# The first eight key and query blocks: from GpSimd's casting loads to fp32 loads on the SyncE and ScalarE queues

## The chip, the cores and the metric

The kernel runs on one core of a Trainium2 chip. A core has TensorE (PE in the profile; PEld is its loading of weights), VectorE (DVE), ScalarE (ACT), GpSimd (POOL) and SyncE (SP), which work side by side and wait for each other by semaphores. SP, ACT and POOL can each start transfers (DMAs) between the chip's memory and the on-chip memory. The metric is the time of one execution on the device in microseconds (us). Less is better.

## The reference, cut to what matters

An attention with 8 batches, 8 heads, 576 positions of 64 numbers, a window of 128 positions and a bias that falls with the distance, and then a two-layer network with a squared relu. Inputs and output are fp32.

```python
batch, n_heads, seq, head_dim = (8, 8, 576, 64)
n_tokens, d_model, d_ff = (4608, 512, 2048)
...
scores = scale * np.matmul(q, k.transpose(0, 1, 3, 2))
bias = slopes[:, None, None] * (-np.abs(rel).astype(np.float32))[None, :, :]
mask = (rel >= 0) & (rel < window)
scores = np.where(mask, scores + bias[None], -1000000000.0)
...
attn = np.exp(scores)
attn = attn / (np.sum(attn, axis=-1, keepdims=True) + 1e-09)
out = np.matmul(attn, v)
...
x = np.ascontiguousarray(attn_out.transpose(0, 2, 1, 3)).reshape(B * S, H * D)
h = x @ w_in
r = np.maximum(h, 0.0)
g = r * r
return (g @ w_out).astype(np.float32)
```

## The kernel before, in words

**Tiles.** All products run in bf16 with fp32 sums. The 4608 tokens are cut into 40 blocks, numbered by m: a block is 128 query positions of one batch (64 for the last of a batch) with all eight heads. For each block its keys and queries (tile kq, 128 positions by 2 x 512 numbers) and values are loaded, keys and queries are transposed (kqT, or kqf for the first four), scores, exponentials and the product with the values follow, the result x is normalized and transposed into xT. Blocks 0 to 3 are the first blocks of four batches. They have no block before them and are handled by `lone`, which adds the bias by a product with the identity. The later blocks multiply by a table of masks.

**Then the network.** Groups g of 512 tokens go through w_in (products h, relu on ACT, square on DVE or ACT, into g) and through w_out (products o, added up, stored). Group 0 and its neighbours are done in small units; later groups with a Strassen-like scheme of seven products, which needs sums of weights (us for w_in, wsum for w_out).

**Names of steps.** `lkq5` loads keys and queries of block 5 by POOL's queue, `lv5` its values; `w_in0` to `w_in4` and `w_out0` to `w_out3` are pieces of the weights, also by POOL's queue, and each casts from fp32 to bf16 on its way. `tp5.0` and `tp5.1` transpose the block's keys and queries on PE (blocks 0 to 7; later blocks by a DMA of SP, `kqT8` and on), `ev5.0.0` evacuates them from PSUM, `b`, `s`, `e`, `pv`, `r`, `n`, `xp`, `x` are a block's bias, scores, exponentials, product with the values, reciprocal, normalization, transposition and its evacuation. `u0.2.1` is the second piece of the w_in products of tokens 256 to 383 of group 0, `reluu0.2.1` and `squ0.2.1` what follows it; `o` are the w_out products of group 0.

**What sets the order.** The program is not ordered by the loops. Every step is a task with engines that may run it, and the string ORDER lists all tasks as they are emitted, with the engine chosen for each (:d DVE, :a ACT, :g POOL, :s SP, none PE) and the PSUM bank or buffer. An engine runs its own tasks strictly in this order, so whatever stands ahead of a task on its engine delays it. A queue's DMAs are issued in order too. Completions of DMAs are counted on eight counters for the two hardware queues and eight for POOL's, so that a DMA can also wait for the one that used its counter before.

**Around the change.** Block 0 alone is loaded otherwise (N_HW = 1): its keys and queries come as fp32 in four loads of 128 KB, `lk0.0`, `lk0.1`, `lq0.0`, `lq0.1`, on SP and ACT, each in runs of 256 numbers (1 KB), into a stage that lies in the memory of wsum before wsum is needed, and DVE casts them into kq (`ck0`, `cq0`). The position on a partition is another one there (four positions of a pair of heads lie together), which the evacuation after the transposition puts right. The source's pattern is

```python
if split:
    return s.rearrange("(c r) (g i) d -> g c r (i d)", r=2, i=4)
return s.rearrange("h s d -> s h d")
```

The load of blocks is at L551 to L600 (`source`, `load_block`), the transposition at L630 to L675 (`transpose_kq`).

Of the kernel before, what the change touches and what calls it, by code (L numbers as in the profile page):

```python
# [8 lines left out]
FP32 = mybir.dt.float32  # L9
# [8 lines left out]
N_HW = 1  # L18
# [24 lines left out]
NF = 8  # L43
UT = 1
# [6 lines left out]
RT = 4  # L51
# [10 lines left out]
s0 tp3.0::5 tp3.1::1 n1.1:d e0.0:a b3::7,0 ev3.1.0:a ev3.0.0:a xp1.0::3 s3 n2.0:d r2.1:d one0.0:d pv0.0::6  # L62
n2.1:d e0.1:a pv0.1::1 x1.0:a xp2.0::2 one0.3:d r0.0:d x2.0:a u0.1.0::5 r0.1:d n0.0:d n0.1:d xp0.0::4 u0.2.0::3
e3.0:a e3.1:a x0.0:d dist0:d u0.0.1::6 u0.0.0::2 pv3.0::1 pv3.1::7 one1.4:d r3.0:d n3.0:d r3.1:d one1.1:d n3.1:d
u0.1.1::0 u0.0.2::4 xp3.0::1 u0.2.1::7 x3.0:d mask1.2:a reluu0.1.1:a:0 reluu0.0.1:a:1 reluu0.2.0:a:2 squ0.0.1:d
squ0.2.0:d u0.3.0::0 reluu0.1.0:a:3 u0.2.2::6 reluu0.2.1:a:1 mask0.3:a reluu0.0.2:a:2 squ0.2.1:d reluu0.2.2:a:1
squ0.2.2:d squ0.1.0:d u0.3.1::3 w_out3:g o0.2.0::1 tp4.0::5 tp4.1::7 squ0.1.1:d one1.7:d ev4.1.0:d squ0.0.2:d
reluu0.3.0:a:1 mask1.5:a mask0.5:a mask1.6:a mask0.6:a reluu0.0.0:a:3 ev4.0.0:a one1.3:d squ0.0.0:d u0.1.2::4
reluu0.1.2:a:0 reluu0.3.1:a:2 us3.0:d one1.0:d u0.0.3::6 reluu0.0.3:a:3 one1.8:d u0.3.2::0 s4::2,7,5,4 mask0.2:a
mask1.3:a mask0.4:a mask0.0:a mask1.0:a e4.0:a e4.3:a squ0.1.2:d squ0.0.3:d mask0.1:a mask1.7:a mask1.1:a  # L70
mask0.7:a reluu0.3.2:a:0 squ0.3.0:d squ0.3.2:d u0.2.3::3 reluu0.2.3:a:3 mask1.4:a one1.6:d squ0.2.3:d e4.1:a
# [24 lines left out]
S2.1.1:d S4.1.1:d S3.1.1:d u2.0.7::6 u2.0.6::2 squ2.0.5:a reluu2.0.6:a:3 e13.2:a reluu2.0.7:a:0 m13.3:d lv16:g
lkq17:g lkq20:g x12:s x10:s x11:s u2.0.4::3 p1.5.0::5 reluu2.0.4:a:1 p1.5.1 s14::4,2,7,6 s5_1:a:5 e14.0:a
e14.1:a e14.2:a m13.2:d m13.0:d m13.1:d S4.1.0:d p1.6.0 pv13.0::3 u2.0.3::4 squ2.0.6:d squ2.0.4:d us1.1:d
m14.1:d r13.0:d m14.2:d n13.0:d m14.0:d reluu2.0.3:a:3 e14.3:a reluu2.0.1:a:1 squ2.0.0:a squ2.0.7:d p1.6.1
pv13.1::2 p1.3.0 r13.1:d n13.1:d m14.3:d s2_1:a:6 s15::7,3,4,6 pv14.0::1 pv14.1::2 r14.0:d r14.1:d us0.1:d  # L100
n14.0:d n14.1:d squ2.0.3:d lv15:g lkq18:g lkq19:g lv17:g lv18:g p1.7.0 p1.7.1 e15.0:a e15.3:a e15.2:a e15.1:a
s16::7,6,1,4 m15.0:d e16.0:a u2.1.2::2 e16.1:a e16.2:a reluu2.1.2:a:0 e16.3:a kqT17:s kqT20:s st1.2.1:s x14:s
x13:s kqT19:s u2.1.0::3 m15.1:d pv15.0::7 u2.1.3::6 reluu2.1.3:a:2 reluu2.1.0:a:3 c22_1:d us0.3:d m16.0:d
m15.2:d m15.3:d pv15.1::1 m16.1:d pv16.0::2 r16.0:d n16.0:d squ2.0.1:d r15.0:d r15.1:d p1.4.0 u2.0.2::4
u2.1.1::6 n15.0:d m16.3:d n15.1:d s17::3,2,7,1 reluu2.0.2:a:1 squ2.1.0:a m16.2:d pv16.1::4 squ2.0.2:d r16.1:d
# [224 lines left out]
def kernel(  # L330
    ctx: ExitStack, tc: tile.TileContext, q, k, v, moe_w_in, moe_w_out, out
):
    nc = tc.nc

    B, H, S, D = q.shape
    d_model = moe_w_in.shape[0]
# [9 lines left out]
    FCB = d_ff // 128  # L346
# [1083 lines left out]
```

## Time and profile before

| | |
|---|---|
| median of three runs | 294.59 us (294.20 to 294.94) |
| profiled execution | 293.89 us, of which the span from first to last instruction is 292.1 |
| PE busy | 282.8 us, 97% of the span |
| DVE, ACT, POOL busy | 247.1, 226.9, 106.5 us |
| granted clock of PE | 1.0 in every slice |
| read from memory | 36.70 MB |
| written to memory | 9.44 MB |
| POOL's queue | 115184 packets, 18.10 MB |
| SP's hardware queue | 54800 packets, 20.26 MB |

The span counts from the first instruction of the program. "Busy" of an engine is the time in which one of its instructions was running; a matmul's end is modelled. In lines of the timeline, the first number is the start and the second the duration; a line with SPq or ACTq is the issue of a transfer by that queue, whose landing comes later; a part in brackets is the idle time of the engine before the line and what ended it. A line number such as L572 is one of the kernel before.

### The profile page before, as it was taken

The page shows a single profiled execution, that of the slowest core. Times are in us where ns is not written, and L with a number is a line of the kernel's source. Part 1 is how long each engine was busy: PE and PEld are TensorE (multiplying, and loading weights), DVE is VectorE, ACT ScalarE, POOL GpSimd, SP SyncE. Part 2 cuts the span into 40 slices and gives each one's busy share as a digit, 9 for nine tenths or more (in the row PEclk, how much of TensorE's full clock was granted, in tenths as well). Part 3 has the DMA queues.
Part 4 walks back from the last instruction along what each step waited for, and adds up shares of the span by engine and source line. Part 5 has one row for each costly group of instructions (what it writes and reads, how often), then busy time and mean ns, then how long its engine had stood idle before and what let it go on. Part 6 is the DMA issues. An engine that isn't in the chain of part 4 may idle for free.

```text
span 292.1 us, 8683 instructions
## 1 busy us (share of the span) xinstructions
PE 282.8 (97%) x3443; PEld 238.5 (82%) x3443; DVE 247.1 (85%) x645; ACT 226.9 (78%) x445; POOL 106.5 (36%) x132
## 2 busy tenths in 40 slices
PE   5889999999999999999999999999999999999994
PEld 2589766788888888888888888888898888888884
DVE  4444588877798699999999999999999898999883
ACT  3658967688789695899999999899886957858710
POOL 8954377393265372912573630820000000000000
PEclk9999999999999999999999999999999999999999
DMA  9999999999999999999999999998500523010225
GB/s 124 166 199 195 190 167 179 145 130 141 180 167 143 179 207 171 131 139 173 185 173 141 142 197 154 168 168 139 116 3 5 152 80 91 1 41 20 90 81 154
DMA packets 170921, 39.64 MB, mean 136 GB/s; under 512 B 156928, under 2 KB 170368, under 8 KB 170880
## 3 DMA queue, kind: packets, MB, share of 16 engines
q0 software_dynamic: 115184, 18.10, 95.1%
q1 hardware_dynamic: 54800, 20.26, 37.6%
q10 hardware_dynamic: 896, 0.72, 1.0%
q8 instruction: 27, 0.44, 0.6%
q14 instruction: 14, 0.11, 0.1%
HBM read 36.70 MB, written 9.44 MB: 158 GB/s over the span
## 4 chain that ended last, share of the span: by engine, by line
PE 87%; DMA 8%; POOL 4%; issue 0%; ACT 0%; DVE 0%; POOLq 0%
PE o L1221 33%; PE h L1059 26%; PE h L965 13%; PE pv L816 6%; PE s L711 5%; DMA vf<-in_v_dram 3%; DMA kqT<-kq 3%; PE o L1137 2%; DMA kq<-in_q_dram 2%; POOL kq L590 2%; POOL vf L597 1%; POOL w_in_sb L535 1%; PE o L1323 1%; PE xp L865 0%; PE tp L653 0%
## 5 line engine op out<-in xcount | busy, mean ns | idle before, releaser
L734 ACT ACTIVATE P<-s 128x512 bf16<-128x512 f32 x120 | 65.6, 612 | 5.2 <-PE s L711 4.9
L1221 PEld LDWEIGHTS <-g 128*128 128x128 bf16 x624 | 60.0, 98 | 7.0
L590 POOL DMA_DIRECT2D kq<-in_k_dram x39 | 33.9, 868 | 69.4 <-DMA kqT<-kq 65.6
L932 ACT ACTIVATE rt<-h 128x512 bf16<-128x512 f32 (+1 forms) x73 | 42.3, 600 | 14.7 <-PE h L965 9.9
L1080 DVE TENSOR_TENSOR rt<-h,f 128x512 bf16<-128x512 f32 x72 | 48.7, 686 | 4.1 <-PE h L1059 1.3
L924 ACT ACTIVATE g<-rt 128x512 bf16<-128x512 bf16 x80 | 48.9, 636 | 1.4 <-DVE rt L1085 0.7
L1221 PE MATMUL o<-w_out_sb,g 128*128 128x256 bf16 x384 | 47.7, 273 | 0.0
L965 PE MATMUL h<-xT,w_in_sb 128*128 128x128 bf16 (+1 forms) x512 | 46.4, 246 | 0.0
L443 ACT ACTIVATE f<-h 128x512 f32<-128x512 f32 x59 | 34.9, 606 | 11.1 <-PE h L1059 10.9
L965 PEld LDWEIGHTS <-w_in_sb 128*128 128x128 bf16 x512 | 38.9, 98 | 3.9
L1059 PE MATMUL h<-xT,w_in_sb 128*128 128x256 bf16 x288 | 41.4, 273 | 0.1
L1059 PEld LDWEIGHTS <-w_in_sb 128*128 128x128 bf16 x384 | 35.8, 98 | 5.2 <-issue 0.3
L742 DVE TENSOR_TENSOR P<-P,masks 128x512 bf16<-128x512 bf16 x96 | 37.1, 420 | 2.2 <-ACT P L734 2.1
L597 POOL DMA_DIRECT2D vt<-in_v_dram x36 | 30.8, 876 | 16.6 <-PE pv L816 9.0
L590 POOL DMA_DIRECT2D kq<-in_q_dram x39 | 33.7, 865 | 5.7 <-DMA w_out_sb<-in_moe_w_out_dram 2.3
L926 DVE TENSOR_TENSOR g<-rt 128x512 bf16<-128x512 bf16 (+1 forms) x65 | 26.1, 415 | 6.9 <-ACT rt L932 6.6
L845 DVE TENSOR_TENSOR x<-pv,rec 128x256 bf16<-128x256 f32 (+1 forms) x80 | 31.4, 414 | 0.5
L1221 PE MATMUL o<-wsum,sums 128*128 128x256 bf16 x256 | 31.7, 273 | 0.0
L1221 PE MATMUL o<-wsum,g 128*128 128x256 bf16 x240 | 30.5, 273 | 0.0
L1059 PEld LDWEIGHTS <-us 128*128 128x128 bf16 x288 | 27.1, 98 | 3.7
L1087 ACT ACTIVATE rt<-rt 128x512 bf16<-128x512 bf16 x38 | 24.1, 637 | 5.6 <-DVE rt L1080 5.2
L816 PEld LDWEIGHTS <-P 128*128 128x128 bf16 (+1 forms) x576 | 24.0, 100 | 5.0 <-issue 2.3
(81 smaller groups left out, 398.3 us busy)
## 6 DMA issues: line engine op xcount, KB each, us to landing
out_dram<-f SPq DMA_DIRECT2D x54, 128.0 KB, 2.6
kq<-in_k_dram POOLq DMA_DIRECT2D x31, 128.0 KB, 5.9
kq<-in_q_dram POOLq DMA_DIRECT2D x31, 128.0 KB, 6.5
vt<-in_v_dram POOLq DMA_DIRECT2D x28, 128.0 KB, 7.0
w_out_sb<-in_moe_w_out_dram POOLq DMA_DIRECT2D x4, 512.0 KB, 14.5
w_in_sb<-in_moe_w_in_dram POOLq DMA_DIRECT2D x3, 512.0 KB, 10.2
out_dram<-f SPq DMA_DIRECT2D x4, 256.0 KB, 5.0
out_dram<-f SPq DMA_DIRECT2D x13, 64.0 KB, 2.1
```

The source lines that it names most:

```text
L443: nc.scalar.activation(o, i, AF.Copy)
L590: nc.gpsimd.dma_start(view(kq[s_kq[m].idx], i), source(src, m, split))
L597: nc.gpsimd.dma_start(tile_of(s_v[m])[0:n, :, 0:D], source(v, m))
L734: nc.scalar.activation(flat(Pt[sP.idx]), sS[i].tile.rearrange("p (j t) -> p j t", j=2)[:, :, lo:hi], AF.Exp, bias=0.0, scale=scale)
L742: nc.vector.tensor_tensor(flat(Pt[sP.idx]), flat(Pt[sP.idx]), flat(masks), op=ALU.mult)
L816: nc.tensor.matmul(sv.tile[0:n, hi * (D + 1):(hi + 1) * (D + 1)], prob, tile_of(s_v[mk])[:, h, 0:D + 1], start=mk == parts[0][1], stop=mk ...
L924: nc.scalar.activation(o, i, AF.Square, bias=0.0, scale=1.0)
L932: nc.scalar.activation(rts[srt.idx][:, 0:n], slot.tile[:, 0:n], AF.Relu, bias=0.0, scale=1.0)
L965: nc.tensor.matmul(slot.tile[:, f * w:(f + 1) * w], w_in_sb[:, cc, fc * 128:(fc + 1) * 128], xT[:, cc, lo % (XR * 128):lo % (XR * 128) + w ...
L1059: nc.tensor.matmul(slot.tile[:, j * 256:j * 256 + 256], a, b_, start=fresh and j == 0 and c == 0, stop=c == 1, skip_group_check=True)
L1080: nc.vector.tensor_tensor(rts[srt.idx], slot.tile, other(), op=ALU.add)
L1221: nc.tensor.matmul(slot.tile[:, z * 256:z * 256 + 256], stationary(c), moving(c), start=fresh and z == 0 and c == 0, stop=c == F - 1, skip ...
```

## The change

The blocks 0 to 7 are now all loaded as block 0 was: 32 loads of 128 KB in fp32, on SP's or ACT's queue, whichever ORDER names. There are four stages instead of one, in the four quarters of wsum; block m uses stage m % 4, so block 4 can be loaded when block 0's casts are done. The casts may run on DVE or ACT. POOL's queue keeps the values, the weights, and the keys and queries from block 8 on. The evacuation of the transposed blocks 1 to 7 takes the order of positions that only block 0 had. ORDER is new from beginning to end: block 1 is now first, then 2, 0 and 3, and the later work has other places, engines and banks.

```diff
-N_HW = 1
+N_HW = 8
...
 ORDER = """
-lk0.0:s iota:g ident:d dist1:d slope1.0:d slope0.3:d one0.1:d lk0.1:a lkq2:g warm0:d slope1.1:d warm::0 lkq1:g
-lq0.0:s slope1.3:a slope1.2:a slope0.2:a ck0:d slope0.0:a slope0.1:a lq0.1:a one0.2:d tp0.0::1 tp2.0::2 tp2.1::3
-ev2.0.0:d ev2.1.0:d tp1.0::4 ev1.0.0:a tp1.1::5 b2::6,7 s2 ev1.1.0:a b1::0,2 s1 b0::3,4 e2.0:a e2.1:a e1.0:a
-e1.1:a ev0.0.0:a cq0:d tp0.1::5 lv2:g pv2.0::6 r2.0:d ev0.1.0:d lv1:g lkq3:g lv0:g w_in0:g w_in1:g w_in2:g lv3:g
-w_in3:g w_out0:g lkq4:g w_in4:g w_out1:g w_out2:g lkq5:g lv4:g pv1.0::7 pv1.1::0 pv2.1::2 r1.1:d r1.0:d n1.0:d
...
+lk2.0:a iota:g ident:d dist1:d slope1.1:d warm0:d lk1.0:s lq1.0:s lq1.1:a lk1.1:a lv0:g warm::0 slope0.3:d
+lk3.0:s lk3.1:s lk0.0:s lv1:g slope1.0:d slope0.2:a slope0.0:a slope0.1:a ck1:d cq1:d ck3:d one0.1:d slope1.3:a
+slope1.2:a b0::1,2 tp1.0::3 tp1.1::4 ev1.0.0:d b1::5,6 tp3.0::7 ev3.0.0:d lk2.1:a lk0.1:a lq2.0:a lv2:g lq2.1:s
+lq0.0:s lq3.1:a lq0.1:a lq3.0:s ck2:d cq2:d ev1.1.0:a s1 e1.0:a b2::0,3 ck0:a e1.1:a pv1.0::4 r1.0:d one0.2:d
+n1.0:d cq0:d tp2.0::7 tp2.1::5 tp0.0::6 tp0.1::4 ev2.0.0:a ev2.1.0:a cq3:a s2 pv1.1::7 ev0.0.0:d ev0.1.0:d
+r1.1:d n1.1:d w_in1:g w_in0:g w_in2:g lv3:g w_in3:g lk4.0:s lq4.1:s lq4.0:s lk4.1:s w_in4:g w_out0:g w_out1:g
+e2.0:a e2.1:a tp3.1::5 ev3.1.0:d s0 pv2.0::6 e0.0:a e0.1:a b3::4,0 pv2.1::7 r2.0:d one0.0:d n2.0:d r2.1:d n2.1:d
+xp1.0::3 pv0.0::5 s3 x1.0:a pv0.1::1 xp2.0::6 u0.1.0::2 r0.0:d n0.0:d r0.1:d n0.1:d xp0.0::7 one0.3:d x0.0:d
+e3.0:a x2.0:a e3.1:a reluu0.1.0:a:0 lk5.0:a mask1.5:a u0.2.0::3 dist0:d u0.0.1::5 u0.0.0::4 pv3.1::1 pv3.0::6
+lk5.1:s mask0.4:a reluu0.0.0:a:1 mask1.4:a u0.0.2::0 u0.1.1::2 r3.0:d r3.1:d n3.0:d n3.1:d xp3.0::7 squ0.1.0:d
+x3.0:d u0.2.1::4 ck4:d u0.3.1::6 u0.3.0::1 lk6.0:s lq6.0:s lq5.0:s lq5.1:s mask1.3:a reluu0.2.0:a:2
...
-    stages = [wsum.rearrange("p s c t -> p (s c t)")[:, 0:4 * d_model].bitcast(FP32)]
+    stages = [x.rearrange("p c t -> p (c t)").bitcast(FP32) for x in (wsum[:, i] for i in range(4))]
...
         if split:
-            s_st = Slot("stage")
             t_l = []
+            s_st = Slot(f"stage{m % 4}")
             for i, src in enumerate((k, q)):
-                for r, (eng, e) in enumerate((("SP", nc.sync), ("SP", nc.sync) if m else ("ACT", nc.scalar))):
-                    def fetch(i=i, src=src, r=r, e=e):
-                        e.dma_start(view(stages[s_st.idx], i)[:, r], source(src, m, split)[:, :, r])
+                for r in range(2):
+                    def fetch(i=i, src=src, r=r):
+                        e = nc.scalar if t_l[2 * i + r].eng == "ACT" else nc.sync
+                        e.dma_start(view(stages[m % 4], i)[:, r], source(src, m, split)[:, :, r])
...
             def cast_kq(i):
                 w = slice(i * d_model, (i + 1) * d_model)
                 copy((c_k, c_q)[i],
                      kq[s_kq[m].idx][:, w].rearrange("s (i r d) -> s r i d", i=4, d=D),
-                     stages[s_st.idx][:, w].rearrange("s (r i d) -> s r i d", r=2, d=D))
-            engs = {"DVE": 350.0, "ACT": 480.0} if m else {"DVE": 350.0}
+                     stages[m % 4][:, w].rearrange("s (r i d) -> s r i d", r=2, d=D))
+            engs = {"DVE": 350.0, "ACT": 480.0}
```

More of the change, by code (lines that the diff above doesn't have):

```diff
@@ L62 @@
[L62 to L71, printed above, removed]
@@ L97 @@
[L97 to L105, printed above, removed]
-p1.4.1 e17.0:a n16.1:d e17.3:a e17.2:a reluu2.1.1:a:1 m17.2:d squ2.1.1:d m17.3:d kqT18:s st1.2.0:s x15:s
@@ new lines @@
+pv12.0::6 r12.0:d n12.0:d m12.2:d squ1.1.4:a reluu1.1.6:a:2 u2.0.6::1 reluu2.0.6:a:1 squ1.1.3:a us0.1:d S1.1.0:d
+u2.0.5::2 squ1.1.6:a S1.1.1:d S2.1.0:d S4.1.0:d S2.1.1:d s13::7,4,5,3 u2.0.0::1 e13.0:a e13.1:a reluu2.0.5:a:0
+reluu2.0.0:a:3 u2.0.4::6 reluu2.0.4:a:2 e13.2:a squ2.0.0:d e13.3:a p1.5.0::7 p1.5.1 m13.2:d s5_1:d:5 m13.1:d
+s14::4,2,1,6 pv12.1::5 r12.1:d n12.1:d m13.0:d e14.0:a e14.1:a squ2.0.5:a e14.3:a lkq17:g lv16:g lv15:g lv17:g
+lkq20:g x11:s x10:s x12:s S4.1.1:d p1.6.0 u2.0.7::3 reluu2.0.7:a:3 squ2.0.7:a pv13.0::4 m14.0:d r13.0:d m14.1:d
@@ new lines @@
+f7.0.2::2 p6.2.0::5 f7.0.5::0 c11.7.0:d:1 s1_6:a:1 sqc12.6.2:a reluc22.6.3:a sqc22.6.3:a st5.2.1:s x35:s
+st5.7.2:s p6.2.1 f7.0.6 s5.7.0:a:0 st5.4.2:s st4.3.0:s st5.7.3:s st5.4.3:s x37:s sqc12.6.3:d S1.6.1:d S2.6.0:d
+ut7.2:d n36.1:d c11_6:d S2.6.1:d S4.6.1:d f7.1.5::1 f7.0.3 s5.7.1:a:6 s2.7.0:a:4 S4.6.0:d c12.7.0:d:3 S3.6.1:d
+st5.3.0:s x36:s st4.3.1:s x38:s st5.3.1:s p6.5.0::2 f7.1.1::3 p6.5.1 st5.2.0:s st6.2.1:s s1.7.1:a:2 p6.6.0
+f7.1.2::5 f7.0.7 f7.1.6 c11.7.1:d:2 S3.6.0:d reluc11.7.0:d reluc12.7.0:a s2.7.1:a:4 sqc12.7.0:a s5_6:a:2
```

278 lines of the change are left out of this document (141 added, 137 removed).

## The prediction

> **What bounds the kernel now.** I read the page's first part, then the windows of the first 50 us, then the chain, the timeline of the start, and the DMA slices of the first 12 us. The page:
>
> ```profile
> PE 282.8 (97%) x3443; PEld 238.5 (82%) x3443; DVE 247.1 (85%) x645; ACT 226.9 (78%) x445; POOL 106.5 (36%) x132
> ```
>
> PE leaves 9.3 us of the span idle. The windows (us; busy of PE, PEld, DVE, ACT, POOL; clock; DMA share; GB/s) say where:
>
> ```profile
> 0.00:5.00 5.00, 2.19 (x6) 0.82 (x7) 2.65 (x10) 2.39 (x6) 4.20 (x10) 1.00 0.71 107
> 5.00:10.00 5.00, 3.52 (x38) 2.21 (x36) 1.69 (x3) 0.78 (x2) 5.00 (x6) 1.00 2.18 157
> 10.00:15.00 5.00, 4.72 (x71) 3.08 (x70) 2.63 (x11) 4.36 (x9) 5.00 (x8) 1.00 1.92 174
> 15.00:20.00 5.00, 4.30 (x79) 4.08 (x80) 1.88 (x8) 3.00 (x7) 2.30 (x4) 1.00 1.45 197
> 20.00:25.00 5.00, 4.87 (x91) 4.87 (x91) 2.54 (x9) 3.13 (x7) 2.44 (x3) 1.00 1.51 194
> 25.00:30.00 5.00, 5.00 (x80) 4.46 (x77) 2.70 (x12) 4.25 (x12) 2.56 (x4) 1.00 1.39 203
> ```
>
> From 25 us on PE is full, so only the first 20 us (and the tail, whose steps stay) can be won. In the chain, the last link of the start is the load of the fourth value block, v3, issued at 11.50 and 8.59 us on its way:
>
> ```profile
> 11.50 8.59 DMA vf<-in_v_dram
> ```
>
> The timeline shows what PE had done when that load let it go on:
>
> ```profile
> 0.74 0.69 SPq L572 DMA_DIRECT2D wsum<-in_k_dram  x1
> 0.74 0.68 ACTq L572 DMA_DIRECT2D wsum<-in_k_dram  x1
> ...
> 3.29 0.57 ACTq L572 DMA_DIRECT2D wsum<-in_q_dram  x1
> ...
> 3.79 0.59 DVE L441 CAST kq<-wsum 128x512 bf16<-128x512 f32 x1 [0.48 <-DMA wsum<-in_k_dram]
> ...
> 7.83 0.92 DVE L441 CAST kq<-wsum 128x512 bf16<-128x512 f32 x1
> ...
> 16.55 1.06 PE L965 MATMUL h<-xT,w_in_sb 128*128 128x128 bf16 x16
> ...
> 17.66 1.95 PE L965 MATMUL h<-xT,w_in_sb 128*128 128x128 bf16 x32
> ...
> 20.13 0.40 PE L816 MATMUL pv<-vf,P 128*128 128x65 bf16 x8 [0.52 <-DMA vf<-in_v_dram]
> ```
>
> At 20.13 the four lone blocks but for block 3's values product, and 48 h matmuls (u0.1.0, u0.2.0, u0.0.1, u0.0.0), are behind PE. The new order has the same list ahead of pv3.1. So the change is worth the shift of this one point, when PE passes pv3, plus whatever goes wrong later. The DMA slices of 0.3 us (window 0 to 12):
>
> ```profile
> GB/s 0 0 0 0 0 0 0 82 273 324 249 226 114 122 167 134 142 139 161 170 184 158 147 173 157 154 155 155 154 155 154 155 155 155 154 155 155 154 155 152
> ```
>
> Fp32 loads of the two hardware queues reach 324 GB/s alone; POOL's casting loads run at 155 GB/s (bytes as written), and the window from 12 to 30 us shows 200 to 210 GB/s where weights move. The engines are never empty after 2.1 us.
>
> **The change part by part, and the sum.**
>
> *POOL.* It loses 14 issues of 0.87 us (12.2 us). Its queue is now v0, v1, v2, w_in1, w_in0, w_in2, v3: three issues of some 0.9 from 1.34 and three w_in issues 0.73 apart put v3's issue at 6.3 instead of 11.50. Behind it stand seven transfers instead of thirteen.
>
> *SP and ACT.* 32 loads of 128 KB instead of 4. SP takes 23: 21 more at 0.58 are 12.2 us on a queue that is otherwise idle until the store at 43.57, so nothing waits but these loads. ACT takes 9, 7 more at 0.57 (4.0 us). Three go out by 2.6; then the table load (1.28, to 3.85) and five slope copies (1.2, to 5.05), then five more loads to 7.9. Only then can ACT start the first evacuation (ev1.1.0), against 8.93 before.
>
> *Casts.* 16 instead of 2: 10 more on DVE at 0.59 to 0.92 (5.9 to 9.2 us), 4 on ACT at the 0.60 of its evacuations (2.4 us). DVE is idle for 21 us and ACT for 17 of the first 50 (windows above and their continuation), which covers them; if it didn't, they would add to engines that are 95% busy from 120 to 200 us. Taken at nothing, except on the chain below.
>
> *The chain of the lone blocks.* Landing takes 2.8 to 3.0 us early, 4.4 once POOL's loads run (ACT's q load, issued 3.29, cast at 7.83). Block 2's k half goes out at 5.05, block 0's at 5.6, block 2's q half at 6.2, block 3's at 6.8, block 0's q half at 7.3: landed 9.4, 10.0, 10.6, 11.2, 11.7. DVE casts block 0's q to 12.4 (r1.0 and n1.0, 0.6 us, stand ahead of it). ACT then runs ev1.1, e1.0, ck0 (from 10.0), e1.1, ev2.0, ev2.1, cq3, two e2, two e0, x1.0 at 0.6 each: it is the busy engine, and x1.0 ends at 16.0. u0.1.0 starts at 16.0 (16.55 before); x2.0 ends at 17.2; u0.2.0, u0.0.1, u0.0.0 (0.89 per 16 matmuls) end at 19.0. By this chain alone PE would pass pv3 at 19.0, 1.1 us earlier.
>
> *v3's landing.* What must have been moved: four v at 0.846 (131 KB at 155 GB/s), 3.4 us; three w_in pieces, 1.05 MB at 205 GB/s, 5.1 us; 16 k and q loads at 0.405 (131 KB at 324 GB/s). Up to 3.6 us some 346 KB (five slices) are gone, 2.6 loads; 13.4 are left, 5.4 us. Sum from 3.6: 17.5. But loads of blocks 4 to 7 no longer stand behind the weights in POOL's queue. SP issues the first when block 0's k is cast (10.6), the second when its q is (12.4), then one each 0.58, and each lands some 4.4 us later whatever POOL has queued: in this trace ACT's load, issued at 3.29 after two of POOL's and while its third was being issued, took 4.4, while POOL's own k loads of the window from 12 to 30 us took a median of 13.5. Nine are issued by 16.5 and landed by 21, 3.6 us more: v3 lands at 21.1 instead of 20.09.
>
> The price of 0.405 is a lower bound: in the six slices from 5.4 to 7.2 us, where ACT's load of 131 KB ran beside POOL's, the total was 139 to 184 GB/s; 298 KB moved where POOL alone moves 279, so it took 0.72 us from POOL. Stores beside POOL's loads later in the trace are no dearer than 0.4. I take 0.405, since it is the rate of queued loads, as these are, and that row is of a single one; the upper end is kept (17.5 becomes 21.7 and n loads cost 0.72 each: eight land by then, 27.5, +7.4).
>
> The Trainium skill (DMA: Bandwidth & Descriptors, "Issuing engines are not separate DMA queues") states that DMAs of all engines run on the same 16 DMA engines and that spreading them saves the sequencer's time only. The trace agrees (139 to 184 GB/s together, 155 alone); by that rule the sum is the bytes' time, as above, and the 12.2 us saved on POOL are worth nothing.
>
> *After pv3.* w_in3 follows with 2.55 and seven more loads (2.8): 26.5. PE needs it for u0.2.2 5.9 us after 21.1 (pv 0.46, five h groups at 0.89, xp 0.39, tp 0.61): 27.0. Covered by 0.5 us. ACT's load of block 5 waits in the built program for the landing of SP's load of block 6 (a shared completion counter): issued 15, landed 19.3; behind it on ACT are masks and the relus that free the banks. PE needs the first of these banks (u0.2.1) after two h groups and xp3, 2.7 us past pv3; not seen in the sum, a loss of up to 1 us if the load takes 7.
>
> *The new order of the rest.* PE's idle time after 25 us is under 0.3 us before, so no gain; the loss is open where DVE has 19.5 to 19.9 of 20 us. Between 0.3 gained and 2 lost I take 0, as the products and buffers are the same.
>
> Sum: 21.1 - 20.1 = +1.0 us. The profiled execution took 293.89 (span 292.1 and 1.8 around it), which would become 294.9; the median of the runs, 294.59, lies 0.7 above it: 295.6.
>
> **The rivals.**
> *Chain sets it (faster).* v3 lands by 19.0: this needs blocks 4 to 7 to stay behind (at most three of them ahead: 17.5 + 1.2). For it: SP waits for casts and completions before it issues. Against: nothing else stands in SP's queue. It decides below 20.1, and gives 293.5.
> *Contended price.* Each load takes 0.72 of POOL's time throughout. For it: the only slices with both kinds of loads. Against: it is one load at a ramp. At 0.55, the middle, v3 lands near 24.4: 298.9; at the end, 302.
> *Nothing.* POOL's queue gets more turns, chain and landing balance near 20.1: 294.6. This is also the case that the move of queues does nothing because the transfers bound both kernels.
>
> **How the numbers follow.** v3 late by about 1 (0.4 to 2.5): 0.46, 295.6. Chain: 0.23, 293.5. Contended: 0.15. Nothing: 0.16. A change under 0.3% (0.9 us) can't be told from none here. Faster by more: 0.23 of the chain case and some order luck, 0.24; same: the nothing case and a little of the first, 0.19; slower: the rest, 0.57. The range leaves out the far end of the contended case and order luck below the chain: 293.2 to 299.0.
>
> **What would show it.** Right: pv3 waits for the DMA of vf, PE idles some 2 us near 19 to 21, block 5 or 6 loads land before v3, x1.0 ends near 16. Wrong: vf lands by 19; or PE waits earlier, for a cast or for ACT's evacuations past 17; or PE shows idle slices after 30 us, where I have none; or w_in takes the place of v3.

## The result, and the profile after

The changed kernel takes 304.17 us (median of six runs, 302.55 to 305.26); the kernel before took 294.76 beside it (293.64 to 295.80). The ratio is 1.0314 (1.0272 to 1.0356): slower by 9.4 us, where 1.0 had been forecast, and above the end of the forecast range, 299.0. The profiled execution took 305.08 us, 11.2 more than the one before.

The first part of the page of the changed kernel, and the line of its second part that gives the clock granted to PE in 40 slices of 7.6 us:

```profile
PE 287.7 (95%) x3432; PEld 241.2 (80%) x3432; DVE 253.3 (84%) x661; ACT 225.5 (74%) x443; POOL 94.2 (31%) x118
PEclk9999699999999999999999999999999999999999
```

PE is busy 4.9 us longer with 11 instructions fewer, and one slice, the fifth, has a lower clock. The windows (busy time and instructions of PE, PEld, DVE, ACT, POOL; clock; DMA share; GB/s) show the stretch:

```profile
5.00:10.00 5.00, 3.62 (x15) 1.59 (x14) 1.90 (x5) 0.48 (x3) 4.35 (x6) 1.00 1.64 227
10.00:15.00 5.00, 2.77 (x35) 1.98 (x34) 1.61 (x4) 2.48 (x5) 1.67 (x3) 1.00 1.29 256
15.00:20.00 5.00, 4.03 (x67) 2.89 (x67) 3.95 (x14) 3.71 (x8) 1.71 (x3) 1.00 1.43 210
20.00:25.00 5.00, 4.92 (x95) 4.79 (x91) 3.29 (x14) 2.35 (x5) 0.19 (x1) 1.00 1.20 237
25.00:30.00 5.00, 0.94 (x17) 0.82 (x15) 1.05 (x4) 0.82 (x4) 0.00 (x0) 0.88 1.18 244
30.00:35.00 5.00, 5.00 (x48) 4.99 (x48) 1.04 (x3) 3.50 (x11) 0.00 (x0) 0.50 1.20 254
```

From 25 to 30 us PE does almost nothing (17 instructions), and from 30 to 35 it is full but finishes 48, at half the clock. From 25 to 30 us the other engines are all but idle too; only the DMA works. The chain of the first 40 us says on what (start, length, what):

```profile
3.40 6.57 DMA wsum<-in_k_dram
...
9.99 6.39 DMA wsum<-in_q_dram
...
16.46 0.44 DVE kq L442
...
19.45 9.04 DMA wsum<-in_k_dram
...
28.59 0.54 ACTq L574
...
29.59 0.37 ACT rt L933
...
30.00 5.28 PE h L966 x48
```

Two things stand here. First, lq0.1 lands at 16.37, and the cast behind it opens the way for block 0. It stands in ACT's queue and was issued only at 9.99, when lk0.0, whose completion counter it shares, had landed (3.40 + 6.57 = 9.97). Second, a load of SP, lk6.0 (issued 19.45), lands only after 9.04 us, and what it lets go is ACT's load lk5.0, whose completion counter it shares. Behind lk5.0 on ACT stand the masks and the relus that free PE's banks. The timeline of ACT (start, length, engine, line, what; the idle time before it and its releaser in brackets):

```profile
21.79 0.60 ACT L933 ACTIVATE rt<-h 128x512 bf16<-128x512 f32 x1
28.59 0.54 ACTq L574 DMA_DIRECT2D wsum<-in_k_dram  x1
29.18 0.51 ACT L482 ACTIVATE masks<-sums 128x128 bf16<-128x128 f32 x2 [6.78 <-DMA wsum<-in_k_dram]
29.59 0.36 ACT L933 ACTIVATE rt<-h 128x256 bf16<-128x256 f32 x1
```

and that of PE over the same time:

```profile
23.53 0.41 PE L817 MATMUL pv<-vf,P 128*128 128x65 bf16 x8
...
30.00 5.28 PE L966 MATMUL h<-xT,w_in_sb 128*128 128x128 bf16 x48 [4.06 <-ACT rt L933]
35.08 0.89 PE L655 MATMUL tp<-ident,kq 128*128 128x128 bf16 x8
```

So pv3 is passed at 23.53 us instead of 20.13 (+3.4), then PE stands for 4.06, and the 48 matmuls after that take 5.28 instead of 2.84 (the same group at full clock, in the runs below): 9.9 us. tp4, the transposes of block 4, is a good mark for it. In the kernel before it began at 26.82:

```profile
26.82 0.61 PE L653 MATMUL tp<-ident,kq 128*128 128x128 bf16 x8
```

There PE had 16 h matmuls (0.89) and four o matmuls (0.87) more behind it than the new order has at this point, so the mark is 25.1 by the new order's list; now it begins at 35.08. The last 1.2 us come later; 0.53 of them are idle time of PE from 120 to 125 us.

### The profile page after: what moved, and what is told of

Read it like the earlier page. It is cut to its first block, busy times and chain, and to the rows that moved or that the text cites. A ratio compares the mean times of both kernels' runs of the same rounds, so it can differ in the third digit from the quotient of the medians.

```text
span 303.1 us, 8692 instructions
## 1 busy us (share of the span) xinstructions
PE 287.7 (95%) x3432; PEld 241.2 (80%) x3432; DVE 253.3 (84%) x661; ACT 225.5 (74%) x443; POOL 94.2 (31%) x118
## 4 chain that ended last, share of the span: by engine, by line
PE 86%; DMA 10%; SPq 2%; DVE 0%; issue 0%; ACT 0%; ACTq 0%; DVEq 0%
PE o L1222 31%; PE h L1060 25%; PE h L966 13%; PE pv L817 6%; PE s L712 5%; DMA wsum<-in_k_dram 5%; PE o L1138 5%; DMA xT<-x 2%; DMA wsum<-in_q_dram 2%; SPq L574 2%; PE tp L655 1%; PE o L1324 1%; PE xp L866 0%; ACTq L574 0%; DVE kq L442 0%
## 5 line engine op out<-in xcount | busy, mean ns | idle before, releaser
L592 POOL DMA_DIRECT2D kq<-in_k_dram x32 | 27.4, 856 | 99.9 <-DMA kqT<-kq 72.8
L933 ACT ACTIVATE rt<-h 128x512 bf16<-128x512 f32 x73 | 42.6, 602 | 16.2 <-PE h L966 7.1
L966 PE MATMUL h<-xT,w_in_sb 128*128 128x128 bf16 (+1 forms) x512 | 49.2, 254 | 4.1 <-ACT rt L933 4.1
L925 ACT ACTIVATE g<-rt 128x512 bf16<-128x512 bf16 x82 | 50.2, 644 | 0.9 <-DVE rt L1086 0.4
L966 PEld LDWEIGHTS <-w_in_sb 128*128 128x128 bf16 x512 | 41.0, 102 | 8.1 <-issue 4.2
L1060 PEld LDWEIGHTS <-w_in_sb 128*128 128x128 bf16 x384 | 35.4, 98 | 4.8
L927 DVE TENSOR_TENSOR g<-rt 128x512 bf16<-128x512 bf16 (+1 forms) x63 | 25.3, 412 | 7.6 <-ACT rt L933 7.1
L817 PEld LDWEIGHTS <-P 128*128 128x128 bf16 (+1 forms) x576 | 24.7, 101 | 5.7 <-issue 2.5
L1088 ACT ACTIVATE rt<-rt 128x512 bf16<-128x512 bf16 x36 | 22.7, 639 | 8.7 <-DVE rt L1081 8.6
L592 POOL DMA_DIRECT2D kq<-in_q_dram x32 | 27.6, 862 | 1.1 <-DMA vt<-in_v_dram 1.0
```

The source lines that it names most:

```text
L592: nc.gpsimd.dma_start(view(kq[s_kq[m].idx], i), source(src, m, split))
L817: nc.tensor.matmul(sv.tile[0:n, hi * (D + 1):(hi + 1) * (D + 1)], prob, tile_of(s_v[mk])[:, h, 0:D + 1], start=mk == parts[0][1], stop=mk ...
L925: nc.scalar.activation(o, i, AF.Square, bias=0.0, scale=1.0)
L933: nc.scalar.activation(rts[srt.idx][:, 0:n], slot.tile[:, 0:n], AF.Relu, bias=0.0, scale=1.0)
L966: nc.tensor.matmul(slot.tile[:, f * w:(f + 1) * w], w_in_sb[:, cc, fc * 128:(fc + 1) * 128], xT[:, cc, lo % (XR * 128):lo % (XR * 128) + w ...
L1060: nc.tensor.matmul(slot.tile[:, j * 256:j * 256 + 256], a, b_, start=fresh and j == 0 and c == 0, stop=c == 1, skip_group_check=True)
```

## The experiments

Theory A: ACT's stop at lk5.0 (head of line: one load with a late counter, relus behind it) and the clock that falls behind it cost some 6 us. Theory A2: the rest is the first chain, late because the loads of blocks 0 to 3 divide the DMA with what GpSimd's queue moves; A3 extends this to blocks 4 to 7. Rivals: the DMA as a whole is the cost and a moved load changes nothing (B), or the new order of all other work is (C). Columns: first w_in matmul (h), landing of the last of the sixteen loads of blocks 0 to 3, start of tp4 (us, profiled execution); median, what it is above the kernel before that ran beside it, and the ratio's interval.

| run | first h | sixteen | tp4 | median | above before | interval of the ratio |
|---|---|---|---|---|---|---|
| before | 16.55 | | 25.1 (see above) | 294.8 | | |
| changed | 20.62 | 16.37 | 35.08 | 304.17 | 9.4 | 1.027 to 1.036 |
| e1 | 21.18 | 16.08 | 29.01 | 298.20 | 3.4 | 1.009 to 1.018 |
| e2 | 20.53 | 16.28 | 32.30 | 302.24 | 7.5 | 1.023 to 1.030 |
| e3 | 22.07 | 16.55 | 33.04 | 302.22 | 7.5 | 1.021 to 1.030 |
| e4 | 21.37 | 16.11 | 29.37 | 297.91 | 3.2 | 1.008 to 1.015 |
| e5 | 20.19 | 15.95 | 28.12 | 298.99 | 4.1 | 1.010 to 1.017 |
| e6 | 21.26 | 15.95 | 29.14 | 300.74 | 5.8 | 1.017 to 1.021 |
| e7 | 22.21 | 16.92 | 30.05 | 301.73 | 6.8 | 1.016 to 1.027 |
| e8 | 17.67 | 12.90 | 31.26 | 300.94 | 6.2 | 1.018 to 1.030 |
| e9 | 19.72 | 13.28 | 28.45 | 300.43 | 5.7 | 1.015 to 1.023 |
| e10 | 22.00 | 16.73 | 29.84 | 298.70 | 4.0 | 1.011 to 1.017 |
| e11 | 19.11 | 13.54 | 29.00 | 300.15 | 4.8 | 1.010 to 1.023 |
| e12 | 17.65 | 13.09 | 27.74 | 298.94 | 3.6 | 1.005 to 1.016 |
| e13 | 16.89 | | 24.91 | 296.55 | 1.8 | 1.004 to 1.008 |
| e14 | 20.52 | 14.91 | 28.52 | 298.48 | 3.7 | 1.008 to 1.017 |
| e15 | 16.45 | | 25.68 | 296.27 | 1.1 | 1.002 to 1.007 |
| e16 | 20.05 | | 30.27 | 300.68 | 5.5 | 1.016 to 1.023 |

First h, landings, tp4 and all waits come from the one profiled execution of a run, which in e4, e7 and e12 took 2.6, 1.3 and 2.4 us more than the median.

**ACT's stop and the clock: e1, e10, e2.** e1 moves one load to SP's queue:

```diff
-... reluu0.1.0:a:0 lk5.0:a mask1.5:a ...
+... reluu0.1.0:a:0 lk5.0:s mask1.5:a ...
```

> One thing against the changed kernel: the load lk5.0 goes to SyncE's queue (it stands ahead of lk5.1 there), so that ScalarE's queue has no load behind block 3. Theory A (head of line: in the changed kernel ScalarE stood 6.78 us at lk5.0, for the landing of lk6.0 on a shared completion counter; its reluu tasks came late, TensorE idled 4.06 us, and the granted clock then fell to 0.50 for 5 us): the 4.1 us and the 2.4 us that 48 matmuls took longer both go, and the kernel takes 297 to 299 us; no idle of TensorE over 1 us between 25.5 and 30 us, granted clock over 0.85 in 30 to 35. Rival B (the loads of blocks 4 to 7 share the DMA with the weights, and something else of theirs then waits just as long): the wait moves to another row, and the kernel stays within 1 us of 304. Rival C (the new order of the rest costs the time): 302 to 304, with the idle spread over later slices.

Measured 298.20, within A's range. The windows of e1, to be set against the two of the changed kernel:

```profile
25.00:30.00 5.00, 5.00 (x93) 5.00 (x91) 3.02 (x9) 3.90 (x12) 0.30 (x1) 1.00 1.19 244
30.00:35.00 5.00, 5.00 (x98) 4.79 (x96) 2.92 (x9) 3.75 (x12) 3.22 (x4) 1.00 1.21 247
```

DMA share and GB/s are nearly the same as before the move; PE and the clock are full. One letter in the order is worth 6.0 us, and B and C fall as explanations of that part. e10 asks whether it was ACT's queue or the counter. The load stays on ACT, but stands ahead of e2.0 and so gets another counter:

```diff
-lk4.0:s lq4.1:s ... e2.0:a ... reluu0.1.0:a:0 lk5.0:a mask1.5:a
+lk4.0:s lk5.0:a lq4.1:s ... e2.0:a ... reluu0.1.0:a:0 mask1.5:a
```

> One thing against the changed kernel: lk5.0 stays in ScalarE's queue, but five activations earlier, ahead of e2.0 instead of behind reluu0.1.0. It then takes the completion counter of a load that landed near 11.5 us (lk2.1's), where the changed kernel's lk5.0 waited for lk6.0's, which landed at 28.5. Theory A (the stop is the wait for that counter, not a load in ScalarE's queue as such): ScalarE does not stop over 1 us between 16 and 30 us, TensorE does not idle there, and the kernel takes 297 to 299.5 us, as with lk5.0 on SyncE's queue. Rival (any load that ScalarE issues in this stretch stops it, because the ring is full): 301 us or more, with a wait of ScalarE of 3 us or more at the new place.

Measured 298.70, within A's range. ACT issues the load at 15.96 us, between two short pieces of work (the timeline of e10):

```profile
15.79 0.60 ACT L444 ACTIVATE kqf<-tp 128x512 bf16<-128x512 bf16 x1 [0.37 <-PE tp L655]
15.96 0.54 ACTq L574 DMA_DIRECT2D wsum<-in_k_dram  x1
16.28 0.62 ACT L444 ACTIVATE kq<-wsum 128x512 bf16<-128x512 f32 x1
```

So the wait on lk6.0's counter at that place was the cost, not a load in ACT's queue as such. e2 leaves the wait and fills PE's gap:

```diff
-x3.0:d u0.2.1::4
+x3.0:d idle::1 u0.2.1::4      # idle: 18 matmuls 128x512 on zeros, result unread
```

> One thing against the changed kernel: ahead of u0.2.1, the first matmul group that waits for ScalarE's late reluu0.0.0, 18 matmuls of 128x512 on zeros go into a free bank, which nothing reads. They last about as long as the idle stretch (3.9 us at 216 ns each) and leave the wait where it is. Theory A (the clock fell because TensorE idled): the idle of 4.06 us is filled, the wait for ScalarE stays and ends at 30.0 us as before, but the 48 matmuls behind it take 2.7 us and not 5.28, and the kernel takes 301.5 to 302.5 us. Rival B (the clock fell for another reason, the load of the DMA or of the other engines at 30 us): granted clock again near 0.5 in 30 to 35, and no gain, 304 to 305 us.

Measured 302.24: 1.9 us less, with ACT's wait still there (6.37 us). The timeline of PE in e2:

```profile
25.74 4.05 PE L631 MATMUL wm<-sums 128*128 128x512 bf16 x18
29.62 2.84 PE L973 MATMUL h<-xT,w_in_sb 128*128 128x128 bf16 x48
```

The same 48 matmuls, begun 0.4 us earlier, take 2.84 instead of 5.28 us when PE was kept at work. So 4.1 of the 6.0 us are the wait and 1.9 (2.4 in the profiled execution) the clock behind it. The Trainium skill (TensorE: Matmul & The Clock Gate, "HAM oscillation — how this bites in real kernels") warns of idle gaps of PE over some 3.4 us, behind which the clock is halved; the gap here was 4.06 us, the clock behind it 0.50, and the trace agrees.

**The first chain: e4, e5, e8.** All three stand on e1 and keep weights out of GpSimd's queue for a while. The means is a memset of one column that the held load overwrites, put behind a step that ends at the wanted time:

```diff
 # e4: behind the cast ck2, ahead of w_in2 (and lv3 ahead of w_in2)
+nc.vector.memset(w_in_sb[:, 0, 512:513], 0.0)
 # e5: behind the cast ck3, ahead of w_in1
+nc.vector.memset(w_in_sb[:, 0, 256:257], 0.0)
 # e8: behind the copy ev3.0.0, ahead of w_in0 (w_in0 ahead of w_in1)
+nc.vector.memset(w_in_sb[:, 0, 0:1], 0.0)
```

> Two things against the run with lk5.0 on SyncE's queue, of one purpose: w_in2 and what follows it in GpSimd's queue start only when the keys of block 2 are cast (a one-column memset behind that cast, which the load overwrites), near 11.5 us instead of 5.6 us, and lv3 goes ahead of w_in2. Theory A2 (the loads of the first four blocks landed 5.3 to 7.3 us after their issue, instead of 2.7 to 3.0, because weights shared the DMA with them): lq0.1 lands at 13 to 14.5 us instead of 16.4, x1.0 ends by 17.5 instead of 20.2, TensorE has lost 1.5 to 2.5 us less by 20 us; the end gains that less what the later weights cost, 0 to 3. Rival (the hardware queues take about 0.9 us per load of 128 KB whatever runs beside them): lq0.1 still lands after 15.5 us, and the kernel is slower than its twin by the delay of w_in2 and w_in3, 1 to 4 us.

Measured 297.91, no different from e1, and lq0.1 landed at 16.11 as there. It tells nothing of sharing: w_in1 and w_in0 were still in GpSimd's queue until 16.3 us, so it was never empty.

> One thing against the run with lk5.0 on SyncE's queue: w_in1 and everything behind it in GpSimd's queue start when the keys of block 3 are cast, near 10.2 us instead of 4.1 us (a one-column memset behind that cast, which the load overwrites). Unlike the run that held w_in2, this leaves GpSimd's queue empty from the landing of v2 (8.7 to 11.5 us there) until about 12 us. Theory A2 (the loads of blocks 0 to 3 landed late because v and weights of GpSimd's queue shared the DMA with them, about 1 us per load of 128 KB while both queues were filled, against 0.4 us when alone): the last of the sixteen, lq0.1, lands at 12.5 to 14 us instead of 16.1, the casts end by 14.5, and the first matmuls on w_in (21.2 us in the twin) start at 18.5 to 20; the kernel 295.5 to 297.5 us. Rival (the two hardware queues give about 1 us per load whatever runs beside them): lq0.1 still at 15.5 us or later, w_in0 lands near 17.5, and the kernel is slower than its twin, 298.5 to 301.

Measured 298.99. Five loads landed between 11.27 and 12.33 us, 0.27 us apart, once v2 was out of the way. Then w_in1 came, and lq3.1 and lq0.1 took until 13.93 and 15.95. The chain gained 0.9 us at tp4, PE waited 0.9 us more near 114 us, and the whole gained nothing that can be told from e1. The rival's numbers came out (landing at 15.5 or later, 298.5 to 301), but not its reason: loads 0.27 us apart are not one per us whatever runs beside them.

> Against the run with lk5.0 on SyncE's queue: w_in0 and all behind it in GpSimd's queue start behind the copy ev3.0.0 (near 11 us, about 2 us later than in the run before it, where the last two of the sixteen loads, lq3.1 and lq0.1, still met the weights and took 1.6 and 2.0 us, while the five ahead of them had landed 0.2 to 0.4 us apart), and w_in0 goes ahead of w_in1. Theory A2 (sharing with GpSimd's queue is what makes the first chain late, the one part of the loss that lk5.0's move leaves): lq0.1 lands by 13 us, its cast ends by 13.6, the first matmuls on w_in start at 16.5 to 18 us if w_in0 is there by then (my estimate: 15.5 to 16.5), against 21.2 in the twin; TensorE has lost 10 to 11 us by 25 us instead of 12.94; the kernel 294.5 to 297 us. Rival (the chain behind the casts, or the later weights, take the gain back): first matmuls on w_in at 19.5 or later, 297.5 to 300 us.

Measured 300.94. The first half of A2 is right: all sixteen landed by 12.90 us, and the first w_in matmul began at 17.67. Its end, 294.5 to 297, was missed by 4 us. The slices of 0.6 us of the DMA's rate from 0 to 24 us, first of the changed kernel:

```profile
GB/s 0 0 0 32 294 283 92 116 171 200 279 220 229 189 233 238 279 272 224 239 278 257 255 256 254 248 207 207 207 176 197 240 210 202 215 239 265 236 234 241
```

then of e8:

```profile
GB/s 0 0 0 43 297 252 94 157 237 228 228 228 198 213 233 277 368 381 377 283 144 166 165 130 141 114 116 177 218 201 208 228 247 224 238 241 237 245 244 246
```

Between 9.6 and 11.4 us the two hardware queues, alone, move 368 to 381 GB/s, where both kinds of queue together move 224 to 279. But from 12 to 16 us e8 moves only 114 to 166: in that stretch the held weights move alone. SP's loads of blocks 4 to 7, issued from 12.57 on, move their first packet at 16.24, and from then on they share the DMA with the weights. v3 lands at 24.57, and PE's timeline in e8 has the wait in the old place:

```profile
18.79 1.95 PE L968 MATMUL h<-xT,w_in_sb 128*128 128x128 bf16 x32
24.70 0.40 PE L819 MATMUL pv<-vf,P 128*128 128x65 bf16 x8 [3.96 <-DMA vf<-in_v_dram]
24.94 2.61 PE L968 MATMUL h<-xT,w_in_sb 128*128 128x128 bf16 x32
```

(32 matmuls after the 3.96 us take 2.61 instead of 1.95: the clock again.)

**Who pays: e9, e11, e16.** e9 is e8 with `lv3:g` ahead of `w_in2:g`; e11 is e9 with twelve of SP's loads, from lk5.0 on, held behind n3.1 in the same way:

> The run e8_weights_behind_later with lv3 ahead of w_in2 in GpSimd's queue: v3 lands 2 to 3 us earlier and w_in2 (512 KB) about 0.9 us later. Theory A2 as there; if v3's landing (near 20.5 us there) is then what stops TensorE at pv3, this run is 0.5 to 1.5 us faster than that one; if w_in2 is what it waits for, up to 1 us slower; if neither, within 0.5 us.

Measured 300.43, 0.5 less than e8, which can't be told from it. v3 landed at 19.89, and then w_in2 was late by 0.55 us and w_out0 by 2.2 (landed 37.4).

> Against e9_v3_ahead: lk5.0 and all loads behind it in SyncE's queue (twelve, of blocks 5 to 7) start behind n3.1, near 23 us instead of 16.3 (a one-column memset behind n3.1, which lk5.0 overwrites). Theory A3 (once blocks 0 to 3 land early, the loads of blocks 4 to 7 and the weights divide the DMA from 14 to 38 us, and the weights come late: w_out0 landed at 37.4 us there and TensorE waited 2.2 us for it, w_in2 0.55 us): w_in2 lands near 21 instead of 23.7, w_out0 2 to 4 us earlier, TensorE waits for neither over 0.5 us, blocks 5 to 7 still in time; the kernel 295.5 to 298 us instead of 300.4. Rival (the same bytes in another order, so that another load is late by as much): a wait for a block 5 to 7 or for w_out1 to w_out3 of 1.5 us or more, 299 to 301 us.

Measured 300.15, and the rival was right in its range and its idea, though not in the loads that it named: PE did not wait for w_out0, but 1.7 us for w_in2 (landed 24.25) and 1.6 for v4. In both runs the loads that were helped came earlier and others came late. e16 goes the other way round: blocks 1 to 3 by GpSimd's queue as before the change, and only blocks 4 to 7 by SP, in the new order with lk5.0 on SP:

```diff
-split = m < N_HW
+split = m == 0 or 4 <= m < 8
```

> Against e15: only the keys and queries of blocks 4 to 7 go by SyncE's queue in fp32 with casts (as in the changed kernel, with lk5.0 on SyncE); blocks 1 to 3 by GpSimd's queue as before. Theory A3 (loads by the hardware queues take DMA time from the weights whichever blocks they are of): sixteen loads from about 11 us on, near 1.1 us each, hold v3, w_in2 and w_in3 back by 2 to 6 us; TensorE waits 2 us or more for them in 18 to 30 us; 297.5 to 301 us. Rival (only the first four blocks matter, blocks 4 to 7 lie beside work): within 1 us of e15.

Measured 300.68, 4.4 above e15, so these loads cost time too. It is also 2.5 above e1, which has all 32 of them. So the price does not go by the number of loads, but by what they hold up: v3 was issued at 6.33 in e1 and at 11.56 here. v3 landed at 25.20 instead of 20.62. (The kernel's own filler put 4.0 us of zero matmuls ahead of the first h here; it lay beside the wait for v3, which came last all the same.) The timeline of PE in e16:

```profile
21.17 1.95 PE L957 MATMUL h<-xT,w_in_sb 128*128 128x128 bf16 x32
25.34 0.40 PE L808 MATMUL pv<-vf,P 128*128 128x65 bf16 x8 [2.22 <-DMA vf<-in_v_dram]
```

How the two kinds share the DMA can be counted in the changed kernel's trace. From 21 to 32 us its queues moved (packets, MB, the time that they took as a share of 16 engines' span; software_dynamic is GpSimd's queue, hardware_dynamic SP's):

```profile
q0 software_dynamic: 1394, 1.38, 74.0%
q1 hardware_dynamic: 1380, 1.27, 43.4%
```

and in e13, without loads by SP, in the same stretch:

```profile
q0 software_dynamic: 3767, 2.16, 139.2%
```

So GpSimd's queue moves 125 GB/s and SP's 115 in the changed kernel, and GpSimd's alone moves 196 in e13. The 9.7 loads of 131 KB that moved in this time took from the weights (196 - 125) x 11 us = 0.78 MB, or 4.0 us at 196 GB/s: 0.41 us a load. In the queue each needed 1.1 us (131 KB at 115 GB/s): lq4.1, lq4.0, lk4.1, lk5.1 and lk6.0, issued from 16.92 to 19.45, landed at 24.20, 24.99, 26.19, 27.29 and 28.49. But lq4.1, the first of them, took 7.28 us, with only lk4.0 ahead of it. The loads that found SP's or ACT's queue empty or all but empty beside weights moved their first packet some 4 us after issue (lk4.0 3.99, lq4.1 4.05, lk5.0 4.19), where the first load of the kernel took 1.5. What holds such a load back was not tried. The Trainium skill (DMA: Bandwidth & Descriptors, "Queues, rings and completion order") says that each of the 16 DMA engines takes turns between the queues that have work, a packet at a time. The trace agrees in this stretch, if the profile's packets are counted: 1394 and 1380, of about 1 KB each. From 6 to 16 us it does not come out so: 3453 packets of GpSimd's, mostly under 512 B, against 880 and 768 of the two hardware queues.

**Order or loads: e3, e7, e13, e15.** e3 and e7 set N_HW = 4: blocks 4 to 7 by GpSimd's queue again. e7 is e3 without the kernel's own filler ahead of tp4.

> The changed kernel with N_HW = 4: blocks 0 to 3 as changed, the keys and queries of blocks 4 to 7 again by GpSimd's queue, cast in flight, in the places that the kernel before gave them (lkq4 behind w_out0, lkq5 behind w_out2, lkq6 and lkq7 behind w_out3); no casts for them, all else in the changed order. Theory A (1.5 us from the late first chain, the rest from ScalarE's stop at lk5.0 and the clock behind it): 296 to 297.5 us, with the first 25 us as in the changed kernel (pv3 at 23.5 us). Rival C (the new order of the rest is what costs): 301 or more. Rival D (the first four blocks by these queues are worth something and only blocks 4 to 7 hurt): below 294.5.

> The run with four blocks by the new queues, without the 56 zero matmuls that the kernel's own filler put ahead of block 4's transposes there (3.3 us, laid out for a load that the planner takes to be late; the two landings are seen at 28.3 and 29.1 us, before the filler began at 29.9). Theory A (the four-block version lost its time to that filler and not to the order): 298.5 to 299.5 us, and tp4 starts near 30 us instead of 33. Rival (tp4 waits for something else, near 33 us): an idle stretch of TensorE in the filler's place, and 301 to 303 us.

Theory A missed in both (302.22 and 301.73). The times lie in the rivals' ranges, but tp4 in e7 is where A has it, and e13 and e15 below put the order's price at 1 to 2 us, so the rivals' reasons are not borne out either. In e3 the filler held tp4 back to 33.04; e7 has it at 30.05, as expected, and yet ends 3.5 us above e1, of which 1.0 is there at tp4. For the rest the trace has only waits further back, which e1 does not have. The waits of PE in e7:

```profile
PE h L1059 <- DVE ut L1028: 1.4, 1, 1.4
PE h L1059 <- DMA xT<-x: 0.8, 1, 0.8
PE h L1059 <- ACT f L443: 0.6, 1, 0.6
```

The first stands near 116 us and is found in other runs too: 0.5 us in the changed kernel, 1.1 in e4, 1.5 in e6, 1.7 in e12; none in e1, before, and e3, which has e7's order and loads but for the filler. What makes it come and go was not tried. e13 has the new order with the old loads: N_HW = 1, blocks 1, 3, 2 ahead of the weights in GpSimd's queue, no filler ahead of tp4. e15 is e13 with `lv4:g` ahead of `w_out2:g` and `lkq5:g`.

> The new order with the loads of before: N_HW = 1, the keys and queries of blocks 1 to 7 by GpSimd's queue, cast in flight (in the sequence that the new order wants: block 1, 3, 2 ahead of the weights, lkq4 behind w_in3, lkq5 behind w_out2, lkq6 and lkq7 behind w_out3), only block 0 by SyncE and ScalarE; no filler ahead of block 4's transposes. Everything else stands in the changed kernel's order. Theory B1 (the loads cost the 3.4 us that lk5.0's move leaves, the order by itself next to nothing): 294 to 296.5 us, first matmuls on w_in by 17.5 us. Theory B2 (the new order costs them): 297 to 299.5 us.

> e13_order_only with lv4 ahead of w_out2 and lkq5 in GpSimd's queue. e13's TensorE waited 1.7 us for v4 (landed 36.8 us) and for no other load of the blocks over 0.5. Theory B1 (the new order costs nothing by itself): v4 lands near 33.5, that wait goes, and the kernel takes 294.5 to 295.3 us, no different from the kernel before. Theory B2 (the order has a cost of its own further back): 295.8 to 297.

Measured 296.55 and 296.27: e13 just outside B1 (its first matmuls as B1 has them), e15 within B2. The front is nearly as before the change (first h at 16.89 and 16.45, tp4 at 24.91 and 25.68, against 25.1). e13 waited 1.7 us for v4. e15 did not, but 1.2 us for v3; the two times can't be told apart. So B2 is right in that the new order has a cost of its own, here 1.1 us (ratio 1.002 to 1.007), of which 0.6 is there at tp4; how much of it is the places that I gave to the loads no run separates. By difference, 2.3 of e1's 3.4 us are left to the new loads.

**Two that tried to mend it: e6, and e12 with e14.** e6 takes lq3.1 and lq0.1 from ACT's queue.

> One thing against the run with lk5.0 on SyncE's queue: lq3.1 and lq0.1 also leave ScalarE's queue for SyncE's, so that ScalarE's first copy out of PSUM (ev1.1.0) no longer stands behind loads that wait for a free completion counter (5.05 us of waiting there, until 10.54). Theory A (ScalarE should hold no load behind work): the copy runs near 9 us, block 1's scores near 9.7 instead of 11.2; but the chain that ends last is block 0's, whose queries land last, so that the end gains 0 to 0.7 us: 297.3 to 298.4. Rival (the stop of ScalarE sets the first chain): the first matmuls on w_in start 1 to 2 us earlier than 21.2, and the kernel takes 296 to 297 us.

It did not do what it was meant to: ACT's next load, lq2.0, now waited for a counter in their stead, and ev1.1.0 ran at 10.51 as before. Measured 300.74, above both ranges. tp4 stayed (29.14); of the 2.5 us above e1, 1.5 are the wait near 116 us, and the rest is not traced. e12 is e7 with the weights held as in e9; e14 lets w_in0 go early and puts lv4 ahead of w_out2.

> Against e7_four_blocks_no_filler (blocks 4 to 7 by GpSimd's queue): the weights start behind ev3.0.0 as in e8 and e9, in the order w_in0, w_in1, lv3, w_in2, w_in3, lkq4, w_in4, w_out0 and on. Theory A2: the first four blocks land by 13.5 us, the first matmuls on w_in start by 19.7 us instead of 22.2, and the kernel gains 1.5 to 3 us: 298.5 to 300.5. Rival (GpSimd's queue, which starts its weights 6 us later, is then the bound): a wait for w_in3, lkq4 or w_out0 of 2 us or more, 301 us or more.

> Against e12_four_blocks_held, which waited 1.8 us for w_in2 and 1.7 us for v4: w_in0 is not held (it starts at 4.1 us), the rest behind ev3.0.0 as there, and lv4 goes ahead of w_out2. Theory A2/A3 (DMA time is what the front of the kernel shares out): the sixteen loads end about 1 us later (14 us), w_in2 about 1.3 us earlier, v4 about 4 us earlier; waits of TensorE for w_in2 and v4 together under 1.5 us; 296 to 298 us. Rival: other loads are then late by as much, 298.5 to 300.

e12, at 298.94, gained 2.8 us on e7, as A2 has it: first h at 17.65 and tp4 at 27.74, with waits of 1.8 us for w_in2 and 1.7 for v4 left. In e14 these two waits are gone, but the sixteen land only at 14.91. At 298.48 it can't be told from e12 and lies between A's range, 296 to 298, and the rival's, which began at 298.5. No version beat the kernel before; e15, which has none of the new loads but block 0's four, comes nearest.

One thing no run separates: the move also made two casting loads of a block into four fp32 ones. By the figures here a block's price in the DMA is about the same, 4 x 0.41 = 1.6 us of GpSimd's queue as against 2 x 0.846 = 1.7 for its own two loads (an estimate; 0.846 is 131 KB at the 155 GB/s of the kernel before). What changed is when they come.

## Why the prediction was wrong

*PE bounds the kernel, and pv3 is the point to compare.* Held. pv3 moved by 3.4 us; in e1 it moved by 3.95 (24.08), tp4 by 3.9 (29.01 against 25.1), and the whole by 3.4.

*Landing takes 4.4 us under load.* This step failed, and the first 3.4 us with it. It took one load's time, of a nearly empty queue, as a constant, and ACT's loads as issued without a wait. From 6 to 16 us the hardware queues moved 150 GB/s beside 96 of GpSimd's: 0.87 us for each load of 131 KB, so the landing depends on how many stand ahead: lq0.1 and the seven still on their way at its issue make 8 x 0.87 = 7.0, and it took 6.39. ACT's last loads waited for completion counters of earlier ones: they were issued from 4.77 to 9.99 instead of 5.05 to 7.3, and ev1.1.0 behind them began at 10.58. lq0.1 had to wait for lk0.0 (landed 9.97) and landed at 16.37, not 11.7. From the end of its cast to the end of x1.0 it then took 3.4 us (16.9 to 20.26), near the forecast 3.6, so x1.0 ended 4.3 us late. e8, which removes the company, has the landing at 12.90.

*v3 lands at 21.1, at 0.405 us a load.* It landed at 20.23, and that it came so near is luck: two errors met. The price held from 21 to 32 us (0.41 us, above). But ahead of v3 nine loads of blocks 4 to 7 were to have landed, and only lk4.0 had. By the prediction's own sum, 20.23 - 3.6 - 3.4 - 5.1 = 8.1 us are left for 13.4 loads and this one, some 0.56 each (an estimate), near the middle price of the contended rival. The prediction had read its six slices from 5.4 to 7.2 us as 139 to 184 GB/s; they are 147 to 184, which changes nothing in its sum. And v3 was no longer what PE waited for. PE waited earlier, for casts, one of the signs that I had named for being wrong:

```profile
PE tp L655 <- DVE kq L442: 4.0, 3, 1.6
```

*ACT's load of block 5: not seen in the sum, up to 1 us.* This step failed by most: 6.0 us (e1). I had found the wait and put its landing at 4.3 us. The load it waits for, lk6.0, was issued at 19.45 instead of 15 and landed after 9.04, at 28.49 instead of 19.3. It was the sixth of SP's loads on the way; six at 1.1 us are 6.6. The rest is the late start above: the second of the six moved its first packet only at 20.97, and landed 3.2 us later. So it is the same wrong constant, with ACT's relus behind it: the wait cost 4.1 us and the clock behind it 1.9.

*The clock* is in no step of the prediction: 1.9 us of these 6.0 (e2). Here a wait of PE of 4.06 us cost more than its length.

*Casts at nothing.* Held as far as a trace shows: in the first 20 us both engines stood waiting for loads and their counters, not for their own casts (DVE 0.44 us of cast behind lq0.1's landing).

*w_in3 in time by 0.5 us.* It landed at 24.79, before the 26.5 forecast, and PE waited for no piece of w_in.

*The new order at 0, between -0.3 and +2.* It has 1.1 us (e15), within the bounds.

*The rivals.* The contended price named the right neighbours, weights and loads in one DMA, and, before v3, about the right price; but the victim was another: the loads came late, and v3 did not. With 3.4 at pv3, 4.1 for ACT's stop and 1.9 to 2.4 for the clock the sum would have been 9.4 to 9.9; the medians differ by 9.4.

## What to carry to other kernels

A load's landing time is not a constant. Here it was, roughly, its place in the queue times the time per load that the queue's share of the DMA gave, and ahead of that, where the queue had run empty beside weights, a start of some 4 us: count what is on its way at that moment, in both kinds of queue. A load in a compute engine's queue stops all work behind it until its completion counter is free, and which load holds that counter must be looked up in the built program and priced with its real landing. When transfers fill the start of a kernel, moving them to other queues may only change which one is late: in e8, e9, e11 and e15 some loads came earlier and another came late.

## What had not been expected of the hardware

- The granted clock also fell without a long gap: in the profiled execution of e4, its slowest, it was 0.50 from 10 to 20 us, where PE's longest idle stretch was 1.5 us (3.40 of 5 us busy from 10 to 15); in e1 0.66 from 15 to 20; in the changed kernel 1.00 from 15 to 20, with about as much idle time from 10 to 20 us as in e1 (6.80 and 6.27 us busy of 10). No run here shows what decides it, and what it cost there is not separated. The 1.00 that a window shows for the first microseconds is no measurement: in the changed kernel two 128x512 matmuls take 1.06 us at 5.88 and at 9.15, and 0.61 at 11.77, and the trace's records of a full clock begin at 11.76 (in the kernel before, at 5.45).
- The two hardware queues alone moved up to 381 GB/s in fp32 (e8), and 224 to 279 together with GpSimd's casting loads in the same 2 us of the changed kernel.
